# The first MLP product of the last two token groups by seven block products, mixed with second products, on one Trainium2 core

## The chip, the cores and the metric

One core of a Trainium2 chip runs the whole program. The metric is device microseconds (us) of one execution, as the median of several.

## The reference, cut to what matters

A linear attention with decay over blocks of 64 positions feeds a two-layer MLP with a tanh gelu:

```python
for b in range(nb):                                   # 12 blocks of 64, 4 batches, 8 heads of 64
    intra = (qb @ kb^T * Dmask) @ vb
    inter = (qb * lam_pow) @ kv_state
    out[:, :, sl] = intra + inter
    kv_state = lam_block * kv_state + (kb * rev_pow)^T @ vb
x = out.transpose(0, 2, 1, 3).reshape(3072, 512)
h = x @ w_in                                          # first product, 512 -> 2048
g = gelu_tanh(h)
return g @ w_out                                      # second product, 2048 -> 512
```

## The kernel before: the parts that the argument touches

The 3072 rows go in seven groups: one of 512 rows, two of 256, four of 512. Attention runs in 24 steps, two of them to a block of 256 rows. From some step on two steps are taken together, called a burst here. MLP work is queued as pieces, and `fill(n)` issues n of them between parts of the attention. In the traces VectorE and ScalarE take their instructions in the order in which the program issues them, even where the first in line has to wait (the copy in k below stands behind a gelu that waits 1.29 us). PSUM is the memory into which TensorE accumulates; the kernel uses it as eight banks.

The first product is plain: four matmuls of 512 columns for each of 16 output tiles of 128, then one ScalarE gelu.

```python
def mm1(fs):
    Hps = ps_M.tile([P, per, N], FP32, tag="M", name="Hps")
    for i, f in enumerate(fs):
        for c in range(NC):                                      # NC = 4
            pin(nc.tensor.matmul(by_block(Hps[:, i, :]), w_in16[:, c, f * P : (f + 1) * P],
                                 x(c), start=(c == 0), stop=(c == NC - 1)))
    ...
    pin(nc.scalar.activation(out=dst, in_=Hps[:], func=AF.Gelu_apprx_tanh))
```

The second product already goes by seven block products (a Strassen scheme: seven products of half-size blocks in place of eight, for some sums of blocks made first). Its operand sums of the gelu's output (`gs`) are made on VectorE, and each product has a half bank of PSUM of its own; VectorE closes the sums.

```python
G_SUMS = {5: ((0, 0), ALU.add, (0, 1)), 2: ((1, 0), ALU.add, (1, 1)), ...}     # five sums
PLACE = {4: ("A", 0), 3: ("A", 1), 5: ("B", 0), 2: ("B", 1), 1: ("C", 0), 7: ("D", 0), 6: ("D", 1)}
def product(m, p):
    ...
    for i in range(HF):
        pin(nc.tensor.matmul(dst, lhsT, rhs, start=(i == 0), stop=(i == HF - 1), ...))
    if m == 2:
        ...                                           # two ScalarE copies, two VectorE additions
    elif m == 1:
        pin(tt(d, banks["C"][:, 0].unsqueeze(1).to_broadcast([P, 2, HE]), d, ALU.add))
    ...
```

The schedule of the last third. `prep(m)` issues what makes step m ready: the scalings of q and k (VectorE and ScalarE) and v (GpSimd), and the DMA transpose of q and k into the tile `qkT`.

```python
prep(18)
for n in range(16, NSTEP, 2):
    burst((n, n + 1), (15,) if n == 16 else (n - 2, n - 1))
    fill(2); U(n); U(n + 1)
    for m in (n + 3, n + 4):
        if m < NSTEP:
            prep(m)
        fill(4 if m % 2 == 0 and n % 4 == 0 else 6 if m % 2 == 0 else 6 if n % 4 == 0 else 10)
```

Of the kernel before, what the change touches and what calls it, by code (L numbers as in the profile page):

```python
# [15 lines left out]
def kernel(  # L16
# [10 lines left out]
    nc = tc.nc  # L27
# [32 lines left out]
    def load_step(s, names="qkv"):  # L60
# [3 lines left out]
        for nm, src in (("q", q), ("k", k), ("v", v)):  # L64
            if nm not in names:
# [13 lines left out]
    w_sum16 = w16p.tile([P, 5, HF, HE], FP16)  # L79
    W_SUMS = {3: ((0, 1), ALU.subtract, (1, 1)), 4: ((1, 0), ALU.subtract, (0, 0)),  # L80
              1: ((0, 0), ALU.add, (1, 1)), 7: ((1, 0), ALU.add, (1, 1)),
              6: ((0, 0), ALU.add, (0, 1))}
    w_slot = {m: i for i, m in enumerate(W_SUMS)}
    wstage = {}
# [35 lines left out]
    def sum_wout(j, m, eng):  # L120

        (f0, e0), op, (f1, e1) = W_SUMS[m]

        def rows(f, e):
            f = f * HF + 4 * j
            return w_out16[:, f : f + 4, e * HE : e * HE + HE]

        pin(eng.tensor_tensor(w_sum16[:, w_slot[m], 4 * j : 4 * j + 4, :], rows(f0, e0), rows(f1, e1), op))  # L128


# [86 lines left out]
    def prep(s):  # L217
        prep_qk(s)
        prep_v(s)
# [140 lines left out]
    def burst(ns, ss):  # L360
# [52 lines left out]
        if i == len(groups[g]) - 1:  # L413
            queue_group(g)
# [47 lines left out]

    groups = [[0, 1], [2], [3], [4, 5], [6, 7], [8, 9], [10, 11]]
# [3 lines left out]
    def queue_group(g):  # L467
# [25 lines left out]
        def mm2(tau, part):  # L493
# [8 lines left out]
            if O2[tau][1] < NF:  # L502
# [8 lines left out]
        G_SUMS = {5: ((0, 0), ALU.add, (0, 1)), 2: ((1, 0), ALU.add, (1, 1)),  # L511
                  1: ((0, 0), ALU.add, (1, 1)), 7: ((0, 1), ALU.subtract, (1, 1)),
                  6: ((1, 0), ALU.subtract, (0, 0))}
        G_PLAIN = {3: (0, 0), 4: (1, 1)}
        W_PLAIN = {5: (1, 1), 2: (0, 0)}
        gsum, pairs = {}, []

        def block(T, F, i):
            return gT[:, i, F, T * HN : (T + 1) * HN]

        def sum_g(i0, i1, ms=None):
            for m, ((T0, F0), op, (T1, F1)) in G_SUMS.items():
                if ms and m not in ms:
                    continue
                if m not in gsum:
                    k = len(gsum)
                    if k % 2 == 0:
                        pairs.append(wst.tile([P, 2, HF, HN], FP16, tag="w32", name=f"gs_{g}_{m}"))
                    gsum[m] = pairs[-1][:, k % 2]
                i = slice(i0, i1)  # L530
                pin(nc.vector.tensor_tensor(gsum[m][:, i, :], block(T0, F0, i), block(T1, F1, i), op))  # L531

        of_pair = {}
        PLACE = {4: ("A", 0), 3: ("A", 1), 5: ("B", 0), 2: ("B", 1), 1: ("C", 0), 7: ("D", 0),
                 6: ("D", 1)}

        def product(m, p):

            banks = of_pair.setdefault(p, {})
            name, half = PLACE[m]  # L540
            final = g == len(groups) - 1 and p == HN // P - 1
            if final and m == 6:
                name = "E"
            if m in (3, 5, 1, 7) or name == "E":
                banks[name] = ps_M.tile([P, 2, HE], FP32, tag="M", name=f"M{name}")
            dst = banks[name][:, half]
            t = slice(p * P, p * P + P)
            for i in range(HF):
                lhsT = block(*G_PLAIN[m], i)[:, t] if m in G_PLAIN else gsum[m][:, i, t]
                if m in W_PLAIN:  # L550
                    F, E = W_PLAIN[m]
                    rhs = w_out16[:, F * HF + i, E * HE : E * HE + HE]
                else:
                    rhs = w_sum16[:, w_slot[m], i, :]
                pin(nc.tensor.matmul(dst, lhsT, rhs, start=(i == 0), stop=(i == HF - 1),  # L555
                                     skip_group_check=True))
            tt = nc.vector.tensor_tensor
            if m == 2:
                o = banks["o"] = otp.tile([P, 2, 2, HE], FP32, tag="o32", name="o32")
                A, B = banks["A"], banks["B"]  # L560
                m525 = mtp.tile([P, 3, HE], FP32, tag="m525", name="m525")
                pin(nc.scalar.activation(out=m525[:, 0:2], in_=B[:], func=AF.Copy))  # L562
                pin(nc.scalar.activation(out=m525[:, 2], in_=B[:, 0], func=AF.Copy))
                flat = o[:].rearrange("p e t d -> p (e t) d")
                banks["diag"] = flat[:, 0:4:3]
                pin(tt(banks["diag"], A[:], m525[:, 0:2], ALU.subtract))  # L566
                pin(tt(flat[:, 1:3], A[:], m525[:, 1:3], ALU.add))
                if final:
                    for T, queue in ((1, nc.sync), (0, nc.scalar)):
                        row = row0 + T * HN + p * P  # L570
                        E = slice((1 - T) * HE, (1 - T) * HE + HE)
                        pin(queue.dma_start(out=out[row : row + P, E], in_=o[:, 1 - T, T, :]))
            elif m == 1:
                d = banks["diag"]
                pin(tt(d, banks["C"][:, 0].unsqueeze(1).to_broadcast([P, 2, HE]), d, ALU.add))
            elif final and m in (7, 6):

                o, T = banks["o"], (0 if m == 7 else 1)
                row = row0 + T * HN + p * P
                rows = out[row : row + P, :].rearrange("q (e d) -> q e d", e=2)  # L580
                d = o[:, T, T, :]
                pin(tt(d, banks[name][:, half], d, ALU.add))
                queue = nc.scalar if m == 7 else nc.sync
                pin(queue.dma_start(out=rows[:, T], in_=d))
            elif m == 6:
                d = banks["diag"]
                pin(tt(d, banks["D"][:], d, ALU.add))  # L587
                for T in range(2):
                    row = row0 + T * HN + p * P
                    pin(nc.sync.dma_start(out=out[row : row + P, :].rearrange("q (e d) -> q e d", e=2),  # L590
                                          in_=banks["o"][:, :, T, :]))
# [32 lines left out]
        for i in range(HF):  # L624
            for fs in ([[i, i + HF]] if per == 2 else [[i], [i + HF]]):
                filler.append(lambda fs=fs: mm1(fs))
        ms = ((3, 4, 5, 2), (1, 7, 6))
        order = [(m, p) for p in range(HN // P) for m in ms[0] + ms[1]]
        if g == len(groups) - 1:
            order = [(m, p) for part in ms for p in range(HN // P) for m in part]  # L630
        for m, p in order:
            filler.append(lambda m=m, p=p: product(m, p))

        def behind(k, i0, i1, ms=None):

            piece = filler[at + k]

            def both():
                piece()
                sum_g(i0, i1, ms)  # L640

            filler[at + k] = both

        at = len(filler) - len(range(HN // P)) * 7 - HF * (2 // per)
        n1 = HF * (2 // per)
        if per == 2:
            behind(5, 0, 4, (5, 2))
            behind(7, 4, 8, (5,))
            behind(8, 4, 8, (2,))
            behind(9, 0, 8, (1, 7))  # L650
            behind(10, 0, 8, (6,))
        else:
            behind(9, 0, 4)
            behind(13, 4, 6, (5, 2))
            behind(n1 - 1, 6, 8, (5,))
            behind(n1, 6, 8, (2,))
            behind(n1 + 1, 4, 8, (1, 7))
            behind(n1 + 2, 4, 8, (6,))

    def fill(n):  # L660
        for _ in range(min(n, len(filler))):
            filler.pop(0)()
# [17 lines left out]
    def U(n):  # L680
        update(n, 1)
# [65 lines left out]
    for m in (6, 3, 4, 1, 7):  # L747
        sum_wout(0, m, DVE)
    sum_wout(1, 6, DVE)
# [4 lines left out]
    sum_wout(1, 3, DVE)  # L754
# [10 lines left out]
    sum_wout(1, 4, DVE)  # L765
# [7 lines left out]
    sum_wout(1, 1, DVE)  # L773
    sum_wout(1, 7, DVE)
# [6 lines left out]
    for n in range(8, 16):  # L781
        stage_t(n)
        fill(1 if n == 9 else 0)
        prep_qk(n + 2) if n == 8 else prep(n + 2)
        fill({9: 1, 14: 3}.get(n, 2))
        R(n, n - 1)
        fill(1)
        U(n)
        if n == 8:
            prep_v(n + 2)  # L790
        fill(2 if n in (8, 11, 15) else 3)

    prep(18)
    fill(2)
    for n in range(16, NSTEP, 2):
        burst((n, n + 1), (15,) if n == 16 else (n - 2, n - 1))
        fill(2)
        U(n)
        U(n + 1)
        for m in (n + 3, n + 4):  # L800
            if m < NSTEP:
                prep(m)
            fill(4 if m % 2 == 0 and n % 4 == 0 else 6 if m % 2 == 0 else 6 if n % 4 == 0 else 10)
    burst((), (NSTEP - 2, NSTEP - 1))
# [29 lines left out]
```

## Time and profile before

| | before |
|---|---|
| time, median of 3 (range) | 203.68 us (203.47 to 204.59) |
| span in the trace | 202.2 us |
| TensorE's last matmul ends | 198.8 us |
| busy: TensorE, VectorE, ScalarE, GpSimd | 194.2, 145.7, 107.9, 66.3 us |
| TensorE's waits after 20 us | 0.16 + 0.34 us |

The row that matters is the last: TensorE hardly ever waits, and the other engines' sums leave room. How full an engine is in one stretch is asked with windows.

Of the tile names in the profiles, `S` are attention's scores, `PT` the masked scores, `Hps` the plain first product, `H` with W, X or Y a bank of the new first product, `M` with a letter one of the second product, `gs`, `xs`, `ws` operand sums, `u`, `q`, `m` copies out of a bank.

### The profile page before, as it was taken

The page shows a single profiled execution, that of the slowest core. Times are in us where ns is not written, and L with a number is a line of the kernel's source. Part 1 is how long each engine was busy: PE and PEld are TensorE (multiplying, and loading weights), DVE is VectorE, ACT ScalarE, POOL GpSimd, SP SyncE. Part 2 cuts the span into 40 slices and gives each one's busy share as a digit, 9 for nine tenths or more (in the row PEclk, how much of TensorE's full clock was granted, in tenths as well). Part 3 has the DMA queues.
Part 4 walks back from the last instruction along what each step waited for, and adds up shares of the span by engine and source line. Part 5 has one row for each costly group of instructions (what it writes and reads, how often), then busy time and mean ns, then how long its engine had stood idle before and what let it go on. Part 6 is the DMA issues. An engine that isn't in the chain of part 4 may idle for free.

```text
span 202.2 us, 5666 instructions
## 1 busy us (share of the span) xinstructions
PE 194.2 (96%) x2348; PEld 130.1 (64%) x2348; DVE 145.7 (72%) x293; ACT 107.9 (53%) x205; POOL 66.3 (33%) x80
## 2 busy tenths in 40 slices
PE   6888999999999999999999999999999999999993
PEld 1456544456888888645688764589664688544882
DVE  5896623889999999967799749899566462334753
ACT  2475778375893473477642368614367424466210
POOL 6594123457458264162531609303302000000000
PEclk9999999999999999999999999999999999999999
DMA  5999999999999999999875999306510003300014
GB/s 170 291 327 387 387 387 378 286 291 320 334 239 216 272 233 235 210 277 200 205 182 127 243 285 218 45 0 138 132 51 3 0 0 107 104 0 0 3 45 163
DMA packets 64201, 37.85 MB, mean 187 GB/s; under 512 B 17584, under 2 KB 59568, under 8 KB 64176
## 3 DMA queue, kind: packets, MB, share of 16 engines
q1 hardware_dynamic: 63344, 36.97, 72.1%
q10 hardware_dynamic: 832, 0.52, 0.8%
q8 instruction: 18, 0.29, 0.6%
q14 instruction: 7, 0.06, 0.1%
HBM read 27.26 MB, written 6.29 MB: 166 GB/s over the span
## 4 chain that ended last, share of the span: by engine, by line
PE 81%; DVE 6%; SPq 4%; DMA 4%; ACT 2%; issue 2%; DVEq 0%
PE Hps L484 37%; PE MB L555 8%; PE MA L555 8%; PE MD L555 7%; SPq L70 4%; PE MC L555 4%; DMA wi<-in_moe_w_in_dram 4%; PE Hps L601 3%; PE O2ps L499 3%; PE S L295 3%; DVE w_sum L128 2%; PE OK L353 2%; PE OK L344 1%; PE Tps L266 1%; DVE gs L531 1%
## 5 line engine op out<-in xcount | busy, mean ns | idle before, releaser
L484 PE MATMUL Hps<-xT,w_in 128*128 128x512 f16 (+1 forms) x416 | 78.7, 346 | 0.0
L488 ACT ACTIVATE gT<-Hps 128x512 f16<-128x512 f32 x88 | 52.3, 597 | 29.1 <-PE Hps L484 28.3
L484 PEld LDWEIGHTS <-w_in 128*128 128x128 f16 x416 | 40.4, 98 | 33.7
L531 DVE TENSOR_TENSOR gs<-gT 128x1024 f16<-128x1024 f16 (+1 forms) x62 | 40.8, 712 | 18.3 <-ACT gT L488 18.3
L456 POOL TENSOR_TENSOR u<-t,lumask 128x256 f16<-128x256 f32 x40 | 29.4, 749 | 67.0 <-DVE t L449 49.6
L555 PEld LDWEIGHTS <-gs 128*128 128x128 f16 x400 | 39.0, 98 | 4.5
L305 DVE TENSOR_TENSOR PT<-S,mask 128x512 f16<-128x512 f32 x48 | 30.4, 682 | 9.5 <-PE S L295 9.5
L230 POOL TENSOR_TENSOR v<-v,dv 128x512 f16<-128x512 f32 x24 | 28.5, 1194 | 5.0 <-DMA v<-in_v_dram 4.5
L555 PE MATMUL MA<-w_sum,gT 128*128 128x256 f16 x160 | 19.5, 273 | 0.4 <-DVE o L587 0.3
L555 PE MATMUL MB<-w_out,gs 128*128 128x256 f16 x160 | 19.1, 273 | 0.0
L248 ACT ACTIVATE qk<-k 128x512 f16<-128x512 f32 x24 | 15.0, 625 | 7.6 <-DMA k<-in_k_dram 7.6
L562 ACT ACTIVATE m<-MB 128x512 f32<-128x512 f32 x10 | 6.0, 597 | 23.4 <-PE MB L555 23.4
L555 PE MATMUL MD<-w_sum,gs 128*128 128x256 f16 x152 | 18.4, 273 | 0.0
L555 PEld LDWEIGHTS <-gT 128*128 128x128 f16 x160 | 15.4, 98 | 3.5 <-ACT gT L488 0.5
L243 DVE TENSOR_TENSOR qk<-q,dq 128x512 f16<-128x512 f32 x23 | 17.6, 767 | 0.0
L430 ACT ACTIVATE xT<-OK 128x256 f16<-128x256 f32 x29 | 11.1, 453 | 8.2 <-PE OK L353 7.9
L499 PE MATMUL O2ps<-w_out,gT 128*128 128x512 f16 x64 | 14.6, 379 | 0.0
L566 DVE TENSOR_TENSOR o<-MA,m 128x512 f32<-128x512 f32 x10 | 6.9, 689 | 9.6 <-ACT m L562 9.6
L128 DVE TENSOR_TENSOR w_sum<-w_out 128x1024 f16<-128x1024 f16 x10 | 9.1, 947 | 6.3 <-POOL w_out L118 3.5
L430 ACT ACTIVATE xT<-O 128x256 f16<-128x256 f32 x18 | 6.4, 458 | 10.4 <-PE O L404 7.5
L295 PEld LDWEIGHTS <-qkT 64*64 64x64 f16 x384 | 6.0, 106 | 7.0 <-issue 3.2
L449 DVE SCALAR_TENSOR_TENSOR t<-t,lamu,OK 128x64 f32<-128x64 f32 x44 | 10.1, 273 | 0.5
(68 smaller groups left out, 168.8 us busy)
## 6 DMA issues: line engine op xcount, KB each, us to landing
q<-in_q_dram SPq DMA_DIRECT2D x24, 256.0 KB, 5.3
k<-in_k_dram SPq DMA_DIRECT2D x24, 256.0 KB, 5.2
v<-in_v_dram SPq DMA_DIRECT2D x23, 256.0 KB, 5.2
out_dram<-o SPq DMA_DIRECT2D x22, 256.0 KB, 4.5
wo<-in_moe_w_out_dram SPq DMA_DIRECT2D x4, 1024.0 KB, 9.6
wi<-in_moe_w_in_dram SPq DMA_DIRECT2D x4, 512.0 KB, 7.6
wi<-in_moe_w_in_dram SPq DMA_DIRECT2D x2, 1024.0 KB, 12.7
v<-in_v_dram ACTq DMA_DIRECT2D x1, 256.0 KB, 4.4
```

Source lines behind the costliest of these rows:

```text
L128: pin(eng.tensor_tensor(w_sum16[:, w_slot[m], 4 * j : 4 * j + 4, :], rows(f0, e0), rows(f1, e1), op))
L230: pin(nc.gpsimd.tensor_tensor(wide(tv[:]), ld32[s][2][:], decay(dv, s), ALU.mult))
L243: pin(q_eng.tensor_tensor(wide(tq), q32[:], decay(dq, s), ALU.mult))
L248: pin(nc.scalar.activation(out=wide(tk), in_=k32[:], func=AF.Copy))
L305: pin(nc.vector.tensor_tensor(t[:, hl].rearrange("p b c d -> p b (c d)"), Sps[:].rearrange("p b c d -> p b (c d)"), mask[:].unsqueeze(1).t ...
L430: pin(nc.scalar.activation(out=d, in_=o, func=AF.Copy))
L456: pin(nc.gpsimd.tensor_tensor(u[:], state[half][:].unsqueeze(2).to_broadcast([P, 2, 2, D]), lumask[:, 2 * half : 2 * half + 2, :].unsqueez ...
L484: pin(nc.tensor.matmul(by_block(Hps[:, i, :]), w_in16[:, c, f * P : (f + 1) * P], x(c), start=(c == 0), stop=(c == NC - 1)))
L488: pin(nc.scalar.activation(out=dst, in_=Hps[:], func=AF.Gelu_apprx_tanh))
L499: pin(nc.tensor.matmul(O2[tau][0][:], gT[:, f % HF, f // HF, tau * P : (tau + 1) * P], w_out16[:, f, :], start=(n == 0), stop=(n == NF - 1)))
L531: pin(nc.vector.tensor_tensor(gsum[m][:, i, :], block(T0, F0, i), block(T1, F1, i), op))
L555: pin(nc.tensor.matmul(dst, lhsT, rhs, start=(i == 0), stop=(i == HF - 1), skip_group_check=True))
```

## The change

The intent: for the last two groups (5 and 6) the first product too goes by seven block products, which saves an eighth of its columns. Four sets, each of two output tiles out of either half, take seven products each. In a set, four products share one bank: product 1 is accumulated on by 6, then by 7, then by 4, and between them the bank's state is copied out or added. The waits this makes for TensorE are to be filled by second products of the group before, cut in halves. The second product takes the same new form everywhere (four operand sums, not five, and the shared bank), steps 16 and 17 run singly, and the last bursts are spread by hand. Cut to its core:

```diff
+    SEVEN = (5, 6)
+    SLOTS = {5: {1: 0, 2: 1, 5: 1, 6: 1, 3: 1, 7: 1}, 4: {1: 0, 2: 1, 5: 0, 6: 1, 3: 1, 7: 1}}
+        X_FACTORS = {1: ((0, 0), (0, 0)), 2: ((0, 1), (1, 0)), 3: (4, (1, 1)), 4: ((1, 1), 4),
+                     5: (1, 1), 6: (2, 2), 7: (3, 3)}
+        def seven(m, k):
+            dst = st[{2: "W", 5: "Y", 3: "Y"}.get(m, "X")]          # 1, 6, 7, 4 share bank X
+            ...                                                     # 2 x 2 matmuls of 256 columns
+            if m == 1:
+                copied("m1", "q32", nc.scalar)
+            elif m == 2:
+                added(0, 0, "m1")                                   # VectorE: m1 += W, gelu later
+            elif m == 5:
+                copied("q", "v32", nc.scalar)
+                release()                                           # the gelus waiting, in order
+            elif m == 6:
+                copied("u2", "k32", nc.vector)                      # must end before 7 may start
+            elif m == 3:
+                added(0, 1, "u2")
+            elif m == 7:
+                added(1, 1, "q")                                    # must end before 4 may start
+            elif m == 4:
+                pending.append(lambda: gelu(1, 0, dst[:]))          # frees bank X
+        def merge(lead, per_set):
+            ...
+            for k in range(HF // 2):
+                for m in (1, 2, 5, 6, 3, 7):
+                    filler.append(lambda m=m, k=k: seven(m, k))
+                    if m == 2 and k > 0:
+                        filler.append(lambda k=k: seven(4, k - 1))
+                    ...
+                    h(slots[m])                                     # old halves between
+            filler.append(lambda: seven(4, HF // 2 - 1))
-    prep(18)
-    for n in range(16, NSTEP, 2):
-        burst((n, n + 1), (15,) if n == 16 else (n - 2, n - 1))
-        ...
+    prep(20)
+    burst((18, 19), (17,))
+    fill(2)
+    U(18); U(19)
+    prep(21)
+    fill(4)
+    prep(22)
+    fill(2)
+    burst((20, 21), (18, 19), 8, 5)
+    fill(3)
+    U(20); U(21)
+    fill(6)
+    prep(23)
+    fill(50)
+    burst((22, 23), (20, 21))
+    ...
```

Cut: the tables and sums of w_in (8 additions, one per step from 8 to 15) and of x, and the new form of `product`, which has the same bank order as `seven`.

## The prediction

> **What bounds the kernel now.** I read the page's busy shares first, then whom TensorE waits for, then the chain that ended last, then the costs of single groups by form.
>
> ```profile
> PE 194.2 (96%) x2348; PEld 130.1 (64%) x2348; DVE 145.7 (72%) x293; ACT 107.9 (53%) x205; POOL 66.3 (33%) x80
> ...
> PE   6888999999999999999999999999999999999993
> ...
> PEclk9999999999999999999999999999999999999999
> ```
>
> TensorE is busy in every slice from the fourth to the last but one, at the full granted clock. Its six largest waits:
>
> ```profile
> PE idle L155 <- DVE ones L149: 1.5, 1, 1.5
> PE Hps L601 <- DVE w_in L108: 0.6, 1, 0.6
> PE Tps L266 <- DVE qk L243: 0.5, 2, 0.3
> PE S L295 <- DVE qkT L271: 0.5, 1, 0.5
> PE Tps L266 <- POOL dq L189: 0.5, 1, 0.5
> PE MA L555 <- DVE o L587: 0.3, 1, 0.3
> ```
>
> By the timeline all lie before 20 us, which the change hardly touches, except 0.16 us of the third line (at 39.7 us) and the last line (0.34 us, ended at 108.0). So after 20 us there is only half a microsecond of waiting to win. A busy TensorE may still be slow; its pace is in the last stretch of the chain of waits, where the pieces lie end to end:
>
> ```profile
> 172.77 13.81 PE Hps L484 x64
> 186.59 1.75 PE MA L555 x16
> ...
> 197.07 0.87 PE MD L555 x8
> 197.94 0.89 PE ME L555 x8
> 198.83 0.02 issue
> 198.85 0.43 DVE o L582
> ```
>
> A matmul of 512 columns takes 13.81 / 64 = 215.8 ns, one of 256 columns 1.75 / 16 = 109.3 ns. There is no slack in that: the kernel is bound by the number of columns. After TensorE's end at 198.8 us come one VectorE addition and a store, to 202.2 us. The other engines' costs, by form:
>
> ```profile
> L488 ACT ACTIVATE gT<-Hps 128x512 f16<-128x512 f32 x88 | 52.3, 597 | 29.1 <-PE Hps L484 28.3
> ...
> L531 DVE TENSOR_TENSOR gs<-gT 128x1024 f16<-128x1024 f16 x38 | 29.6, 836 | 9.7 <-ACT gT L488 9.7
> ...
> L566 DVE TENSOR_TENSOR o<-MA,m 128x512 f32<-128x512 f32 x10 | 6.9, 689 | 9.6 <-ACT m L562 9.6
> ...
> L575 DVE TENSOR_TENSOR o<-MC,o 128x512 f32<-128x512 f32 x10 | 6.8, 682 | 0.2 <-PE MC L555 0.2
> ...
> L563 ACT ACTIVATE m<-MB 128x256 f32<-128x256 f32 x10 | 3.8, 377 | 0.0
> ```
>
> The idle times on the right, and windows of the last fifth of the run (DVE about half busy, ACT about 45%), say that both have room there. Between 50 and 80 us it is otherwise: VectorE is 95 to 100% busy in each window of 10 us, and still TensorE does not wait.
>
> **What the Trainium skill says.** "TensorE: Matmul & The Clock Gate", part 1, gives the warm start-to-start time as N / 2.4 GHz plus about 2.5 ns; 215.8 and 109.2 ns follow for N = 512 and 256, and the trace agrees to a tenth. So halving the width costs only 2.6 ns for each pair. The same page (part 2, on LDWEIGHTS) says the next weights load while a matmul runs; the trace has 98 ns for a load, under 109, and the second products already run so at full pace. "PSUM — Partial Sum Buffer", the section on bank collisions, asks to guard PSUM by bank: TensorE must not write a bank while another engine reads it. That makes the accumulate, copy out, accumulate again of the new scheme a strict sequence; no run so far shows it. "ScalarE: Activation LUTs", under the cost of a load, has back-to-back ACTIVATEs overlapping by about 93 ns; here two gelus of 597 ns at distance zero took 1.31 us together at one place and some 0.5 us apart at others, so I take 0.5 us each.
>
> **The change, part by part.**
>
> First product of the last two groups. Before: 16 x 4 = 64 matmuls of 512 columns, 13.81 us a group. After: 4 sets of 7 products, each 2 x 2 matmuls of 256 columns, 112 x 109.2 ns = 12.23 us. That is 1.58 us less per group, **3.16 us in all**, every bit of it on TensorE's path. It is an eighth less columns, minus 0.02 us a set for narrower matmuls.
>
> Second products. The number of TensorE instructions stays (7 x 8 per pair of row blocks); the seven are only of another form (four sums in place of five, partial results kept in a bank). TensorE: 0. VectorE: per group of 512 rows the operand sums go from 10 to 8 instructions of 128x1024, and the closing additions from 8 of 0.69 us to 2 (4.1 us less). ScalarE: 4 copies become 9 (about 2 to 3.6 us a group).
>
> Attention steps 16 and 17 now run singly, not as a pair. From the chain, a pair costs 1.38 us (with one old step) or 1.82 us; a single step 1.03 us. Before 1.38 + 1.82, after 2 x 1.03 + 1.38: **0.24 us more**.
>
> Work added for the sums. Of w_in: 8 VectorE additions of 128x1024, 0.84 us each or 6.7 us, one per step from 8 to 15, just where VectorE was full. Against them stand, in the same stretch, one w_out sum (0.95), a fifth of the operand sums and most of the closing additions of three groups (about 2.9 us for each small one, 5.8 for the third): a net relief of some 3 to 4 us. Of x: 4 more per group. In each of the eight sets: 3 additions of 0.69 us and a copy of about 0.65 on VectorE, 2 extra copies of 0.6 on ScalarE. Over the run VectorE comes to about 145.7 - 8.2 - 19.5 - 1.8 + 6.7 + 6.7 + 21.4 = 151 us, ScalarE to about 107.9 + 9 + 8 = 125 us. Both are far under TensorE's 190, so neither becomes the bound as a whole; what counts is the order inside a set.
>
> The order inside a set, laid out in units of one product or half product (0.437 us). In group 6 (4 old halves mixed in, 11 units = 4.80 us): product 1 ends at 0.44, 2 at 0.87, the late 4 of the set before at 1.31, 5 at 2.18. Then ScalarE copies 5 (to 2.8), and does four gelus at 0.5: to 4.8. The last of them reads the bank that the next product 1 but one opens, at 4.80. Into that fall ScalarE's copies of the mixed second products (0.3 to 0.6 us a set). So this chain overruns by about **0.45 us** in the sets 2 and 3 where a bank is used again: 0.9 us. In group 5, with 5 halves (5.24 us a set), about 0.15: 0.3 us. The other sequences fit: product 3 needs 5's copy 0.9 us after 5's end, product 7 needs 6's copy 1.3 us after, the late 4 needs 7's addition 1.3 us after.
>
> Handovers. The attention burst between the groups needs eight banks just when the seven-product scheme holds four; group 6 starts with four x copies (1.4 us) and then VectorE sums behind a lead of only 4 halves (1.75 us), and VectorE comes there with a backlog of four score maskings (2.5 us) and three operand sums. I set **0.3 to 0.8 us** for these together.
>
> The end. After the last product a ScalarE copy of 128x256 (0.38) and a store of 128 KB replace an addition (0.43) and the same store: 0.
>
> Old waits after 20 us that may go: VectorE has one w_out sum less before 39.7 us and much less to do at 108 us: **0.5 us** less.
>
> Sum: 203.68 - 3.16 - 0.5 + 0.24 + 1.2 (sets) = 201.46, and with some 0.5 for the handovers 202.0; as the layout looks tuned by hand to where TensorE waits (the uneven filling counts), I cut the new waits by about a third and put the time at **201.4 us**.
>
> **Rivals.** (a) All waits hidden: 203.68 - 3.16 - 0.5 + 0.24 = 200.3 us. For it: TensorE never waited for a full VectorE before. Against: the gelu chain above has no slack. There is no way to 199.6 us (2% faster) by this sum; it would need a shorter head or tail. (b) A new wait takes the whole gain: ScalarE's order. It does all four gelus of a set in one batch; if an old copy stands ahead of them, each set loses 0.5 to 1 us, and 8 sets give 3 to 5 us back: 203 to 205 us. For it: two engines pass each bank to and fro. Against: ScalarE has 3.6 us of work per set of 4.8 to 5.2. (c) VectorE becomes the bound between 60 and 110 us through the w_in sums, and attention steps wait for masked scores: 1 to 3 us more, 202.5 to 204.5. For it: windows at 100% there. Against: the net relief worked out above. (d) Single-row-block groups (1 and 2), where product 7's copy and product 4 follow each other in one bank: the filling counts put an attention step between them, so I expect at most 0.5 us.
>
> **Range and chances.** The lower end is rival (a), 200.3. The upper end lets (b) or (c) take back all but little of the gain: 203.4. Faster by over 2% needs 199.6 or less, below the floor of the sum: 0.03. Slower by over 2% is 207.8, which needs 7 us of new waits: 0.04. The rest, 0.93, is within 2%.
>
> **What would show it.** TensorE's count should be 2348 - 128 + 224 = 2444, its busy time about 3 us less, with L555's 560 matmuls still 273 ns each and the pace of 109 ns in the new product's rows. VectorE near 151 us, ScalarE near 125. Among TensorE's waits I expect a row on ScalarE's gelu (the bank opened by product 1) of about 1 us, small rows at the start of group 6 on the x sums, and the wait on the closing addition at 108 us gone. Waits that last more than 3 us in sum after 20 us would prove the layout of a set wrong; a pace over 112 ns in the new products would prove the column count wrong; TensorE waiting for masked scores between 60 and 110 us would speak for (c). If the span falls by more than 4 us, something outside this list was won.

## More of the kernel before

```profile
120.28 9.66 PE L484 MATMUL Hps<-xT,w_in 128*128 128x512 f16 x44
...
135.98 0.64 PE L295 MATMUL S<-qkT 64*64 64x128 f16 x32
```

From 120.3 to 136.0 us TensorE has 15.7 us of MLP work that needs nothing from the attention. Whatever prepares the next burst has that long.

Of the kernel before, from 120 to 143 us (columns: window, its length, then busy time and instructions of each engine, granted clock, DMA share and rate):

```profile
core 0: us, PE busy (x) PEld busy (x) DVE busy (x) ACT busy (x) POOL busy (x), PEclk, DMA share, GB/s
120.00:143.00 23.00, 23.00 (x259) 16.36 (x257) 20.95 (x42) 12.47 (x26) 9.43 (x11) 1.00 0.48 111
```

VectorE is already 91% busy here (20.95 of 23.00 us), while TensorE never waits.

## The result, and the profile after

The kernel after took 206.64 us (median of 4, 205.84 to 206.71); the kernel before, on the same chip, 204.06 (4 runs). The ratio is 1.011 (95% interval 1.007 to 1.015). Ratios here are those of fast runs alone, and not quite the ratio of the medians quoted. The predicted range, 200.3 to 203.4, did not hold it: where 2.3 us were to be saved, 2.6 were lost. Two later repeats were milder, at 1.0035 and 1.0055 (below); over all 14 runs of the kernel after the median is 205.76, over all 34 of the kernel before 204.1.

The page of the kernel after, busy sums and two rows of the forty slices:

```profile
PE 193.4 (94%) x2444; PEld 140.6 (69%) x2444; DVE 154.7 (76%) x298; ACT 122.5 (60%) x245; POOL 74.3 (36%) x85
...
PE   6988999999998999999999999698999999999992
DVE  5887722589999889959897359999567996679620
```

TensorE's count is the predicted 2444. A dip to 6 now stands in the slice at 128 to 133 us, and around it VectorE's digits read 9. Whom TensorE waits for after 60 us (sum, times, longest):

```profile
PE S L318 <- DMA qkT<-qk: 1.9, 1, 1.9
PE MX L597 <- DVE gs L567: 0.8, 1, 0.8
PE HX L688 <- DVE q L709: 0.7, 2, 0.4
PE HX L688 <- DVE u L701: 0.7, 1, 0.7
```

The longest is a row that the prediction doesn't have: the scores of step 21 wait for a DMA transpose. The chain of waits of the same kernel shows how (start, duration, what):

```profile
121.50 3.48 PE Hps L520 x17
124.97 5.59 DMA qkT<-qk
130.56 0.04 issue
130.60 0.42 PE S L318 x16
```

The transpose is issued at 124.97 and lands at 130.56, after 5.59 us; TensorE would have come to these scores at 128.7 us. The query of step 21 had to be scaled by VectorE first, 123.89 to 124.82 us, after the maskings of the burst before. Between the two bursts there are now 8 pieces (2 + 4 + 2), from 121.3 to 128.3 us: 7 us of work, where the kernel before had 15.7. The same window as shown before, of the kernel after:

```profile
120.00:143.00 23.00, 20.49 (x299) 13.74 (x296) 22.22 (x41) 14.29 (x28) 10.57 (x11) 1.00 0.63 132
```

VectorE went from 91% to 97% busy, and TensorE lost 2.5 us of 23.

To compare traces I use the stretch from the first 512-wide matmul of the first group's plain first product to the end of TensorE's last matmul, called **the stretch** below: before 24.73 to 198.83, so 174.10 us; after 25.52 to 201.21, so 175.69. It leaves out two things. The start: over 17 traces of programs that are the same up to there, that first matmul came between 24.5 and 26.3 us (see the last section). And the end after TensorE: 3.4 us before, 3.6 to 3.7 us in the kernel after and all variants with its second product.

**A ledger.** The change's own terms as predicted, without new waits, put the stretch at 174.10 - 3.16 (columns) - 0.50 (old waits gone) + 0.24 (single steps) = 170.68 us. If that holds, what is above it must be the new waits. I read each from TensorE's timeline, as the listed wait, or among the new products as the start-to-start distance less the regular 0.437 us of four matmuls (a listed wait there is 0.16 us short, since the end of a matmul is modelled; short ones are not listed at all). The rows for the masking and for group 1 are listed waits, and so may be 0.16 us short.

| wait of TensorE | after, first trace | after, repeats r / s |
|---|---|---|
| scores of step 21 for the DMA transpose (128 us) | 1.85 | 0.66 / 0.64 |
| first product after that burst, for VectorE's masking | 0 | 0.23 / 0.26 |
| group 5, first set: product 7 for VectorE's copy of 6 (`u`) | 0.82 | 1.72 / 1.71 |
| last set of groups 5 and 6: product 4 for 7's addition (`q`) | 0.56 + 0.51 | 0.56 + 0.50 / 0.57 + 0.50 |
| group 6: product 1 for the gelu that frees its bank | 0.27 + 0.26 | 0.27 + 0.27 / 0.26 + 0.26 |
| group 1: a second product for a VectorE sum (65.8 us), in s for a ScalarE gelu (60.4 us) | 0.78 | 0 / 0.23 |
| sum | 5.05 | 4.21 / 4.43 |
| 170.68 + sum | 175.73 | 174.89 / 175.11 |
| the stretch, measured | 175.69 | 174.71 / 175.03 |

The ledger closes within 0.2 us, and within 0.4 if the listed waits are taken as 0.16 us longer. So the saving of columns was real, and it was eaten by waits that the prediction had put at about 1.1 us. Two of the rows trade with each other: over after, its repeats and c, d, e below, the transpose took 5.46 to 5.59 us and cost 1.83 to 1.85 where `u` cost 0.82 to 0.95, and took 4.3 to 4.5 us and cost 0.64 to 0.87 where `u` cost 1.72. The sum with the masking's wait stays between 2.6 and 2.8 us: what TensorE does not wait for at 128 us it waits for at 142, where VectorE's queue sets the time.

### The profile page after: what moved, and what is told of

It reads as the page before. It is cut to its first block, busy times and chain, and to the rows that moved or that the text cites. A ratio compares the mean times of both kernels' runs of the same rounds, so it can differ in the third digit from the quotient of the medians.

```text
span 204.9 us, 5961 instructions
## 1 busy us (share of the span) xinstructions
PE 193.4 (94%) x2444; PEld 140.6 (69%) x2444; DVE 154.7 (76%) x298; ACT 122.5 (60%) x245; POOL 74.3 (36%) x85
## 4 chain that ended last, share of the span: by engine, by line
PE 84%; DVE 6%; ACT 4%; DMA 3%; issue 1%; POOL 1%; DVEq 0%
PE Hps L520 22%; PE MX L597 15%; PE O2ps L535 7%; PE MY L597 6%; PE HX L688 6%; PE MW L597 4%; PE S L318 4%; PE Hps L778 3%; DMA qkT<-qk 3%; PE HY L688 3%; PE Tps L289 2%; PE OK L376 2%; PE idle L178 2%; ACT gT L705 2%; PE OK L367 2%; PE HW L688 2%
## 5 line engine op out<-in xcount | busy, mean ns | idle before, releaser
L520 PE MATMUL Hps<-xT,w_in 128*128 128x512 f16 (+1 forms) x288 | 51.0, 332 | 0.0
L524 ACT ACTIVATE gT<-Hps 128x512 f16<-128x512 f32 x56 | 33.3, 596 | 11.8 <-PE Hps L520 11.2
L597 PEld LDWEIGHTS <-gs 128*128 128x128 f16 x320 | 31.2, 98 | 4.6 <-DVE gs L567 1.1
L597 PEld LDWEIGHTS <-gT 128*128 128x128 f16 x240 | 23.2, 98 | 3.5 <-ACT gT L524 0.5
L597 PE MATMUL MX<-w_sum,gs 128*128 128x256 f16 x160 | 21.6, 273 | 0.8 <-DVE gs L567 0.8
L567 DVE TENSOR_TENSOR gs<-gT 128x1024 f16<-128x1024 f16 (+1 forms) x24 | 18.8, 792 | 1.1 <-ACT gT L524 1.0
L688 PEld LDWEIGHTS <-ws 128*128 128x128 f16 x128 | 12.5, 98 | 2.3 <-issue 0.8
L614 ACT ACTIVATE u<-MX 128x256 f32<-128x256 f32 x18 | 6.8, 384 | 9.8 <-PE MX L597 9.8
L318 PE MATMUL S<-qkT 64*64 64x128 f16 x384 | 10.0, 225 | 2.4 <-DMA qkT<-qk 1.9
L567 DVE TENSOR_TENSOR gs<-gs,gT 128x1024 f16<-128x1024 f16 (+1 forms) x12 | 10.6, 881 | 0.3
```

The costliest lines, as they stand in the source:

```text
L318: pin(nc.tensor.matmul(Sps[hl][half64(c), hp, jk, :], o[half64(hl), 1, jk, hp, half64(c)], o[half64(hl), 0, :, hp, half64(c)], start=True, ...
L567: pin(nc.vector.tensor_tensor(g_rows(m, i), g_rows(a, i), g_rows(b, i), op))
L597: pin(nc.tensor.matmul(dst, lhsT, rhs, start=(opens and i == 0), stop=(closes and i == HF - 1), skip_group_check=True))
L688: pin(nc.tensor.matmul(dst[:, i, :], w_in_block(a, slice(c, c + 1), slice(f * P, f * P + P))[:, 0], x_block(b, slice(c, c + 1))[:, 0], sta ...
```

## The experiments

The theory: the gain is there, and six waits, each with its own cause in the schedule, take it. The rival: the form itself is at fault (a bank passed between three engines; VectorE full), so that a wait mended in one place comes back in another. Each of the first four kernels mends one cause. All ran beside the kernel before; b, b2, f, h ran on another chip than the rest, so are best compared by the ratio. "Stretch" is as above; the last column is the ledger, where I drew it up.

| run | time, us | ratio to before (95%) | stretch | 170.68 + its waits |
|---|---|---|---|---|
| a: transpose early | 204.61 | 1.0041 (0.998 to 1.010) | 174.28 | 174.65 |
| c: weight sums later | 204.88 | 1.0026 (0.999 to 1.006) | 174.72 | – |
| d: the bank's gelu first | 205.10 | 1.0043 (1.000 to 1.009) | 175.24 | 175.16 |
| e: last set spaced | 205.46 | 1.0066 (1.002 to 1.012) | 174.89 | 174.81 |
| b: no seven in the first product | 205.19 | 1.0061 (1.002 to 1.010) | 174.54 | – |
| b2: only the new second product | 207.73 | 1.0177 (1.014 to 1.022) | 176.23 | – |
| h: a + v not scaled on GpSimd (wrong result) | 204.26 | 0.9994 (0.995 to 1.004) | 172.88 | 173.26 |
| f: a, c, d, e and more room for step 23 | 203.92 | 1.0010 (0.997 to 1.005) | 173.49 | 173.66 |
| r: the kernel after again | 205.26 | 1.0035 (0.998 to 1.009) | 174.71 | 174.89 |
| j: seven in group 6 alone | 205.20 | 1.0013 (0.995 to 1.008) | slow trace | – |
| k: relieved further | 203.86 | 0.9962 (0.991 to 1.001) | 173.01 | 172.88 |
| k2: relieved, seven in group 6 alone | 202.87 | 0.9938 (0.989 to 0.999) | 172.51 | – |
| s: the kernel after a third time | 205.54 | 1.0055 (1.001 to 1.010) | 175.03 | 175.11 |
| m: relieved, no seven in the first product | 204.05 | 0.9984 (0.994 to 1.003) | 173.42 | – |
| n: k2 again | 203.43 | 0.9942 (0.990 to 0.999) | 172.51 | – |
| o: relieved, two sums behind | 202.33 | 0.9907 (0.985 to 0.996) | 171.79 | 171.74 |

### a: the transposes ahead of the burst

```diff
-qkp: bufs=4, ptp: bufs=3
+qkp: bufs=5, ptp: bufs=2          # SBUF is full: the fifth qkT tile is paid with a masked-score tile
-    prep(20)
+    prep_qk(20); prep_qk(21); prep_v(20)
     burst((18, 19), (17,))
 ...
-    prep(21)
+    prep_v(21)
```

> The query and key preparation of step 21 is moved ahead of the burst of steps 18 and 19 (a fifth buffer for transposed operands, paid for with one of the three buffers of masked scores). Theory 1 (the 1.85 us that TensorE waits at 128.7 us is only the lateness of that DMA transpose, 5.6 us in flight against 7 us of work between the bursts): the wait on the transpose goes, nothing takes its place, and the median falls from 206.6 to about 204.8 us. Rival (the wait only moves): the four maskings come earlier, but VectorE's backlog of operand sums then makes the first set of the new product wait longer than its 0.66 us at 142.7, and the time falls by less than 0.8 us.

The transpose's wait was gone, 1.85 to 0. Yet the stretch fell only by 1.4 us against the first trace of after (0.8 of it is the wait at 65.8 us, absent here too) and by 0.4 against r, because the wait for `u` was 1.72 us, as in r and s and not 0.82, and 0.64 us came up after the burst, for VectorE's masking of scores. TensorE came sooner to a VectorE that was no further on. The cause of the first wait is shown; its worth is small as long as VectorE is the next to be waited for.

### c: the sums of w_in two steps later

```diff
-        if n < 16:
-            sum_win((n - 6) // 2, n % 2, nc.vector)
+        if n >= 10:
+            sum_win((n - 8) // 2, n % 2, nc.vector)
```

> The eight VectorE additions on the w_in blocks run in steps 10 to 17 in place of 8 to 15. Theory 1 (the 0.78 us wait at 65.8 us for an operand sum is there because a w_in sum of 1.53 us stands in front of it on VectorE): the wait is gone or under 0.2 us, median about 205.9 us. Rival (VectorE is full from 60 to 110 us anyway): the wait turns up one group later, at 75 to 110 us, and the time stays within 0.3 us of 206.6.

The wait of 0.78 us at 65.8 us was gone. But it is also absent from a, e, f, k and both repeats of after, which have the sums where they were or moved, and present in d. So it comes and goes by itself, and this run decides nothing.

### d: the gelu that frees the bank goes first

```diff
-                pending.append(lambda: gelu(1, 0, dst[:]))
+                pending.insert(0, lambda: gelu(1, 0, dst[:]))
```

> In each batch of four gelus the one that reads the PSUM bank of product 1 but one is done first, not last. Theory 1 (in the last group TensorE waits 0.27 us at 177.7 and again at 182.8 for just that gelu): both gaps vanish, median lower by about 0.5 us, 206.1 us. Rival (ScalarE as a whole is late there, the order does not matter): the gaps stay or come back at the next product that needs a copy, and the time stays at 206.6.

This wait isn't among the listed ones. ScalarE and TensorE of the kernel after in group 6 show it; first ScalarE, the end of a batch of four gelus:

```profile
176.84 0.62 ACT L705 ACTIVATE gT<-m 128x512 f16<-128x512 f32 x1
177.36 0.59 ACT L705 ACTIVATE gT<-HX 128x512 f16<-128x512 f32 x1
```

then TensorE, product 1 of the next set but one, which opens the bank that the last gelu reads:

```profile
177.28 0.60 PE L597 MATMUL MY<-w_out,gs 128*128 128x256 f16 x4
177.99 0.60 PE L688 MATMUL HX<-xT,w_in 128*128 128x256 f16 x4
```

The bank's gelu is the fourth of the batch and ends at 177.95; product 1 starts at 177.99, which is 0.27 us after its place at 177.28 + 0.44. With the order changed both such gaps, 0.27 and 0.26, were gone, and the other waits of these sets stayed. So the cause of these two is shown.

### e: product 4 of the last set further behind 7

```diff
-                    h(slots[m])
+                    h(slots[m] + (k == HF // 2 - 1) * {2: -1, 7: 1}.get(m, 0))
```

> In the last set of each group one half product of the old group moves from before product 5 to between product 7 and the closing product 4, so that the closing product starts 0.87 us after product 7's end and not 0.44. Theory 1 (the waits of about 0.5 us at 159.3 and at 187.9 are the 0.7 us addition between products 7 and 4): each falls to under 0.15 us, together some 0.8 us, median about 205.8 us. Rival (VectorE is behind by more than that there): the waits stay above 0.3 us each and the time stays within 0.3 us of 206.6.

The gaps of 0.56 and 0.51 us before the last product 4 were gone. Between 7 and 4 there had been one half product, 0.44 us, against an addition of 0.7; now there are two. The second was taken from elsewhere in the set, and other waits appeared: 0.59 us in group 5, for ScalarE's copy `u` in the second product's own shared bank, and 0.22 in group 6. So 1.07 us became 0.81: mostly moved, as the rival has it.

### b and b2: what the new second product costs by itself

```diff
# b
-    SEVEN = (5, 6)
+    SEVEN = ()                    # and no sums of w_in; fill(50) -> fill(22)
# b2: the same, and the kernel before's schedule of steps from 8 on
```

> The new kernel with its order of attention steps and its new second products, but the first product of the last two groups again as 64 matmuls of 512 columns, without the w_in sums. Theory 1 (the seven products do save TensorE 3.16 us, and waits for VectorE and ScalarE inside their sets, some 2.2 us, plus the sums' load eat most of it): TensorE works 3.2 us more, the waits at the new products are gone, the wait of about 1.9 us on the transpose stays, and the time lies within 1 us of the new kernel's. Rival (the column count does not save what was worked out): the time falls below the kernel before's or by over 2 us.

> The kernel before with only the second products in the new form (four sums, separate banks, copies on ScalarE); attention order and first products as before. Theory 1 (the form of the second products takes nothing from TensorE and only relieves VectorE): within 0.5 us of the kernel before, and no wait of over 0.4 us after 20 us. Rival (a bank that is accumulated into again after a copy makes TensorE wait): waits on ScalarE's copies, over 1 us in sum, and 1 to 2 us slower than before.

The kernel b is the kernel after without its point, and its stretch, 174.54, is as long as that of r and s: putting the seven products in, worth 3.16 us by the count of columns, won nothing. The transpose's wait stood in b too, at 0.54 us (1.9 expected), with 0.35 for the maskings: these two belong to the new order of bursts and not to the seven products. With b2, the new second product in the old schedule, the stretch grew by 2.1 us over before. TensorE's timeline of b2 names the waits; one of them:

```profile
66.93 1.03 PE L597 MATMUL MX<-w_sum,gT 128*128 128x256 f16 x8 [0.47 <-ACT u L614]
```

Products 7 and 4 follow each other in one bank, with ScalarE's copy between: the strict sequence that the prediction drew from the Trainium skill's bank rule ("PSUM — Partial Sum Buffer") is now seen, at 0.47 us. In the bursts at 107 and 138 us the attention's matmuls waited another 0.7 and 0.9 us for VectorE's maskings, which by the program free the score banks; that they are short because the new form holds banks across its products is argued, not shown. From b2 to b only the order of steps and filling changes, and the stretch falls by 1.7 us. So the new form did need another order, and it is that order which took the transpose's cover away.

### f: all four mended, and room for step 23

a, c, d and e, and:

```diff
-    fill(6); prep(23); fill(50)
+    fill(21); prep(23); fill(35)
```

> The early transpose, the w_in sums two steps later, the bank's gelu first, the last set spaced, and the preparation of step 23 moved 15 pieces later, behind the first set of the new product. Theory 1 (each wait comes back whole): 206.6 - 1.8 - 0.8 - 0.5 - 0.8 - 0.7, about 202.0 us, 1% below the kernel before. Theory 2 (VectorE is full from 120 to 143 us, so part of it only moves): 202.7 to 203.7 us, with a wait on VectorE of over 0.5 us left in the first set of group 5. Rival (the waits shift and nothing is won): over 204.5 us.

The stretch was 173.49, 0.6 us under before; by time the two are the same (1.0010). Of its waits 1.11 us were for `u`, 0.80 for maskings, 0.59 and 0.48 in later sets. Mending was no illusion, but VectorE stayed.

### h: is it GpSimd beside it that makes VectorE late?

a, and in `prep_v`, for a result that is wrong on purpose (relative error 0.30):

```diff
+        if s in (21, 22, 23):
+            pin(nc.scalar.activation(out=wide(tv[:]), in_=ld32[s][2][:], func=AF.Copy))
+        else:
             pin(nc.gpsimd.tensor_tensor(wide(tv[:]), ld32[s][2][:], decay(dv, s), ALU.mult))
```

> The early transpose, and besides the scaling of v of steps 21 to 23 taken off GpSimd: ScalarE copies v unscaled (a wrong result on purpose). Theory 2 (from 120 to 143 us VectorE is the bound, and its operand sums there take 0.95 to 1.53 us in place of 0.68 because GpSimd works beside them): those sums beside the v scaling fall to about 0.7 us, the first set's wait of 1.55 us shrinks by over 1 us, and the time falls by about 1 us against the early transpose alone (204.6). Rival (the sums are slow for another reason, or the chain is not VectorE's): the sums stay at 1 us and more, or the wait stays.

VectorE's operand sums after the burst, in a, and GpSimd's scalings of v beside them:

```profile
124.08 2.94 POOL L253 TENSOR_TENSOR v<-v,dv 128x512 f16<-128x512 f32 x2
124.70 1.42 DVE L567 TENSOR_TENSOR gs<-gT,gs 128x1024 f16<-128x1024 f16 x1
126.04 1.53 DVE L567 TENSOR_TENSOR gs<-gT 128x1024 f16<-128x1024 f16 x1
```

and the same two sums in h, with nothing on GpSimd after 124.9 us:

```profile
126.21 0.69 DVE L570 TENSOR_TENSOR gs<-gT,gs 128x1024 f16<-128x1024 f16 x1
126.82 0.68 DVE L570 TENSOR_TENSOR gs<-gT 128x1024 f16<-128x1024 f16 x1
```

The same instruction on the same shapes takes 0.68 us alone and up to 1.53 us beside GpSimd. "SBUF — State Buffer" of the Trainium skill, section "Who interferes with whom", says that a VectorE instruction with two SBUF inputs contends with a GpSimd instruction that reads SBUF. The trace agrees, with these numbers; the lock that the page describes isn't visible in it. The stretch fell by 1.4 us against a (by the ratio to before, 0.5%, with intervals that overlap): the 0.64 us for the maskings went, and the wait for `u` fell from 1.72 to 1.05, less than the 1 us expected. Against the repeats of after no other single edit did as much, and the prediction had costed every such sum at the mean of 0.84 us, or less.

### r and s: the kernel after again

> The changed kernel once more, unchanged, for the spread of a second trace. If the waits are set by the program: TensorE again waits 1 to 2 us for the transpose of step 21, 0.4 us twice for the last set's addition and 0.6 us or more for the first set's copy. The 0.8 us wait at 65 us, absent in two of the four variants that do not touch it, may or may not be there. Median 205.5 to 206.7 us.

> The changed kernel a third time, unchanged. If the first figure holds: 206 to 206.7 us and 1% slower than before; if the second: 205 to 205.6 us and 0.4% slower. By either, TensorE waits over 0.6 us for the transpose of step 21 and over 0.6 us for the first set's copy, and the two together over 2 us.

Both repeats were 1.1 to 1.4 us faster than the first measurement, and the ledger above shows where their traces differ by 0.7 to 1.0: the transpose's wait was 0.65 in place of 1.85 us, and the wait at 65.8 us absent, while the wait for `u` grew from 0.82 to 1.71. No gain, and a loss of 0.4 to 1.1% (r's interval alone does not leave out 1). In s, VectorE's queue ahead of that copy, and the product that waits for it:

```profile
135.90 0.98 DVE L567 TENSOR_TENSOR gs<-gs,gT 128x1024 f16<-128x1024 f16 x1
136.92 1.42 DVE L567 TENSOR_TENSOR gs<-gT,gs 128x1024 f16<-128x1024 f16 x1
...
139.46 0.67 DVE L709 TENSOR_TENSOR m<-HW,m 128x512 f32<-128x512 f32 x1
140.06 0.67 DVE L567 TENSOR_TENSOR gs<-gT 128x1024 f16<-128x1024 f16 x1
140.66 0.68 DVE L701 COPY u<-HX 128x512 f32<-128x512 f32 x1
```

```profile
141.39 0.60 PE L688 MATMUL HX<-xs,ws 128*128 128x256 f16 x4 [1.55 <-DVE u L701]
```

The copy has no idle time before it: it isn't late because product 6 was late, but because it stands in line behind operand sums of group 4, four in this batch, three of them longer than 0.68 us. That at least two of the four can be issued later is shown by o below.

### j: seven products in the last group alone

```diff
-    SEVEN = (5, 6)
+    SEVEN = (6,)                  # fill(50) -> fill(24)
```

> Seven block products in the last group only; group 5 multiplies as before, attention order and second products as in the changed kernel. Against the variant with none (205.2 us): theory (the products save 1.58 us a group, and it is group 5's set, run while VectorE is full, that gives it back): 1.58 less, plus about 1.0 us for the two bank waits and the last set's addition, so 204.4 to 204.9 us; the wait for the first set's copy is gone. Rival (each group loses what it saves by its own sets): 205.2 us or more.

The runs spread from 204.06 to 207.24 us. This is inconclusive; k2, n and o ask the same without the other waits.

### k: the copy moved to ScalarE

c, d and e; both transposes and both v scalings of steps 20 and 21 ahead of the burst; step 22 and 23 prepared later; the last store on another queue; and the copy of product 6 in the first set on ScalarE:

```diff
-                copied("u2", "k32", nc.vector)
+                copied("u2", "k32", nc.scalar if k == 0 else nc.vector)
```

> All mends (203.9 us), and VectorE relieved from 120 to 143 us: step 22 prepared later, behind the first sets; v of step 21 scaled before the burst; the first set's product 6 copied out by ScalarE; and the last store issued from ScalarE's queue. Theory 2 (VectorE's full stretch is what is left of the loss): the waits of 0.8 us after the second burst and 0.95 us in the first set fall under 0.3 us each, median 202.2 to 202.9 us, about 0.8% faster than the kernel before. Rival (the wait moves to another engine or to the next set): 203.5 us or more.

ScalarE's timeline of k:

```profile
139.72 0.63 ACT L705 ACTIVATE gT<-m 128x512 f16<-128x512 f32 x1 [1.29 <-DVE m L709]
140.25 0.58 ACT L699 ACTIVATE u<-HX 128x512 f32<-128x512 f32 x1
```

The copy now stood behind a gelu that itself waited 1.29 us for a VectorE addition, so TensorE waited 0.96 us for ScalarE in place of VectorE. An emptier engine didn't help, because its queue is in order and its next instruction hung on the full engine. Still, the transpose's wait and that for the maskings were gone, and the stretch was 173.01. The store's queue changed nothing: 3.7 us after TensorE's end as ever.

### k2, m, n, o: how much the seven products win once the rest is mended

All four are on k's schedule (the counts of pieces fitted to each), the copy back on VectorE. In m no first product by sevens (and no sums of w_in), in k2 and n (one kernel) those of group 6, in o both groups, and two operand sums of group 4 issued behind the first set:

```diff
# o
-            for k, m in ((0, 1), (1, 2), (2, 4), (4, 3)):
+            for k, m in ((0, 1), (1, 2), (2 if w == 1 else 5, 4), (4 if w == 1 else 7, 3)):
```

> Seven block products in the last group only, with the same mends. Theory 2: 1.58 us less saved than with both groups but no first set in VectorE's full stretch: 203.0 to 203.8 us, behind the version with both groups by 0.5 to 1.5 us. Rival (group 5's seven products never pay): it is the faster of the two.

> No seven products at all, with the new second products, the new attention order and the mends that apply (early transpose, v of step 21 early, step 22 late, last store from ScalarE's queue). Theory (the last group's seven products pay about 1.58 us less 0.4 us of waits when mended): 1.0 to 1.3 us slower than the version with the last group only, about 204.0 us. Rival (the mends alone made the gain): equal to it within 0.4 us.

> The version with seven products in the last group only and all mends, once more beside the others: 202.6 to 203.3 us, 0.4 to 0.8% faster than before.

> Both groups by seven products with the mends, product 6 of the first set again copied by VectorE, and two of group 4's operand sums (2.1 us of VectorE's time beside GpSimd) issued behind that set. Theory 2 (the wait of 0.96 us there is only VectorE's queue, in order, with sums ahead that nobody needs yet): the wait falls under 0.2 us and the time to 202.3 to 203.0 us, at or below the version with the last group only. Rival (the sums are needed soon after, so the wait comes back at the third or seventh second product): a wait of over 0.5 us there, 203.5 us or more.

VectorE of o around the same copy:

```profile
137.83 0.67 DVE L709 TENSOR_TENSOR m<-HW,m 128x512 f32<-128x512 f32 x1
138.92 0.69 DVE L701 COPY u<-HX 128x512 f32<-128x512 f32 x1 [0.42 <-PE HX L688]
139.53 0.68 DVE L567 TENSOR_TENSOR gs<-gT,gs 128x1024 f16<-128x1024 f16 x1
```

and its window from 120 to 143 us:

```profile
120.00:143.00 23.00, 23.00 (x325) 16.35 (x325) 19.84 (x41) 14.58 (x29) 9.83 (x12) 1.00 0.37 83
```

Now VectorE waits 0.42 us for product 6, not TensorE for VectorE, and the sum that was stretched to 1.42 us takes 0.68. VectorE is 86% busy with as many instructions as in the kernel after, and TensorE full. Of all waits two are left in this half of the run: 0.58 us for the second product's copy in group 5 (156.3 us) and 0.48 for `u` in group 6 (183.9).

By the stretch, m to n (seven in group 6) wins 0.9 us and n to o (in group 5, with the sums behind) 0.7, where the columns alone would give 1.58 each; by time 0.6 and 1.1 us. From m to o that is 1.6 us, and with o's two waits of 1.06 us 2.7 of the 3.16 us of the columns are seen. The ledger's base without seven products would be 170.68 + 3.16 = 173.84; m, which has no listed wait, took 173.42, so the base is right to about 0.4 us. So the step from m to n lay between its theory (1.0 to 1.3 us) and its rival (under 0.4). And k2 came out faster than k, as the rival that group 5's seven products never pay has it; o, with the sums moved, answers that. The kernel o is the fastest seen: 202.33 us, 0.93% under before with an interval that leaves out 1, and 3.2 us under s of the same rounds.

## Why the prediction was wrong, point by point

- **The bound and the column count: right.** The new products run at 0.437 us for four, 109 ns each; 2444 instructions; and the ledger closes only with the full 3.16 us in it. The old wait at 108 us was gone, as foreseen. TensorE's busy sum fell by 0.8 us and not by 3; some of each wait counts as busy, since ends are modelled, and the start was 0.8 us longer, but the difference was not worked out.
- **Loads of the other engines: nearly right as sums, and misleading.** ScalarE came to 122.5 us (125 predicted), VectorE to 154.7 (151). "Both are far under TensorE's 190, so neither becomes the bound as a whole" was true and beside the point: between 120 and 143 us VectorE was 97% busy, and the bank that four products share hangs on its copy and its addition there. (Two readings were loose, without effect on the sum: VectorE's windows from 50 to 80 us read 94 to 100%, and "the last fifth" is rather the last 55 us.)
- **"Handovers", the step that failed.** The prediction set "0.3 to 0.8 us" for the burst and the start of a group, then cut all new waits by a third. What stood there measured 2.67 us in the first trace (1.85 for the transpose, 0.82 for `u`) and 2.6 in the repeats (0.66 + 0.23 + 1.72 in r). Two terms make it up. The transpose was not foreseen: the prediction counted banks and sums across the new bursts, but didn't ask what the shorter stretch between two bursts (7 in place of 15.7 us) had been hiding. And VectorE's backlog was named, for group 6, but the worst place was group 5, whose start the prediction doesn't cost; the operand sums there were costed at 0.84 us or less, and measured up to 1.53 beside GpSimd. In o, with those sums out of the way, the wait was zero.
- **"The other sequences fit": false in the first and the last set.** "The late 4 needs 7's addition 1.3 us after" holds where three pieces stand between, which the last set doesn't have; there only one half product, 0.44 us, stands between 7 and 4, and 0.56 + 0.51 us went. "Product 7 needs 6's copy 1.3 us after" was reckoned from an idle VectorE. By the prediction's own sign, over 3 us of waits, the layout of a set would be proved wrong; of the 5.05 us, 2.4 lie inside the sets (3.3 of 4.21 in r).
- **ScalarE's gelu chain: right in kind, too large.** Predicted 0.9 + 0.3 us; measured 0.53 in group 6 and none in group 5. Experiment d removed just these.
- **Rivals.** (b), a new wait takes the whole gain, came true in its outcome, by VectorE and a DMA rather than ScalarE's order. (c) was at most the 0.78 us at 65.8 us, which comes and goes. (d) wasn't seen in the kernel after and was 0.47 us in b2 (0.64 from start to start), about its bound of 0.5. (a), all hidden, was not reached even by o.
- **The end: 0 predicted, 0.3 measured**, and not explained: 3.7 us after TensorE's end in place of 3.4 in the kernel after (3.6 to 3.7 in all that have its second product), whichever queue stores.
- **The sum.** New waits after the cut were about 1.1 us; they measured 4.2 to 5.05, so 3.1 to 3.9 us too few. With the 0.3 at the end, 201.4 becomes 204.8 to 205.6, against medians of 205.3, 205.5 and 206.6. The rest lies in the start of the run, which is longer or shorter whatever the kernel.

What stays open: why the wait at 65.8 us comes in some runs; why the transpose takes 5.59 us in one trace and 4.3 in the repeats; what the end's 0.3 us is; and which part of a's wait for maskings is the missing buffer (k and o have it missing too, and do not wait).

## What to carry to other kernels

A kernel whose TensorE never waits holds slack that no page shows: before moving work, ask of each stretch that gets shorter which transfers and which queue of another engine ended inside it unseen. When an accumulator is passed to and fro between engines, cost the passing engine's instruction from its place in that engine's queue, at the duration it has beside its neighbours, not from its own length on an idle engine. And if a saving doesn't show, write the ledger of waits: here it closed within 0.4 us in ten traces and led, by order and one exchange of buffers, to a version 0.9% faster than the kernel before.

## What the Trainium skill lacked or had wrong

- "SBUF — State Buffer" and "GPSIMD Engine Reference" name the contention between VectorE with two SBUF inputs and GpSimd, but give no duration of a VectorE sum under it. Here one of two fp16 tiles of 128x1024 took 0.68 us alone, 0.95 to 1.53 us beside GpSimd's scaling and masking.
- "DMA: Bandwidth & Descriptors" gives a bandwidth for a DMA transpose, no time from issue to landing: here the chain shows 5.59 us for one `qkT` tile, the median of 15 being 4.8 us in the kernel before and 4.0 us in the kernel after.
- "Perfetto Trace Analysis" says that a matmul's end is modelled; it doesn't say that gaps hide behind it. Here gaps of up to 0.27 us are in no list of waits, and listed ones read 0.16 us short; the distance from start to start shows them.
- "TensorE: Matmul & The Clock Gate" calls the warm-up variable and under 1% of a span. The spread of the start here is of that size (the stretch began between 24.5 and 26.3 us, 0.9% of the run), but whether it is the warm-up isn't shown, and 1.8 us is as much as the effects studied here. Eight transposes at 5.42 us took 0.79, 1.03 and 1.34 us in three traces, while the granted clock reads 1.00 in all three, so no view shows that it was the clock.
